# Sliding-window attention and a squared-ReLU MLP on one core: 64-column TensorE tiles, finer first units, token-by-token Q/K loads, V copies inside their partitions

## The chip, the cores and the metric

The kernel runs on one NeuronCore of a Trainium2 chip. The metric is device time in microseconds, the median of several executions. A profile is one more execution, recorded instruction by instruction. The engines are PE (TensorE, matmul; PEld is its weight load), DVE (VectorE), ACT (ScalarE), POOL (GpSimd, here mostly the issuer of casting loads from DRAM) and SP (SyncE, here the issuer of stores and of copies within SBUF).

## The reference

```python
def _attn_ref(q, k, v):            # 8 batches, 8 heads, 576 tokens, 64 wide, float32
    scores = scale * np.matmul(q, k.transpose(0, 1, 3, 2))      # scale = 1/8
    mask = np.abs(pos[:, None] - pos[None, :]) <= 32
    scores = np.where(mask, scores, -1000000000.0)
    ... softmax over the last axis ...
    return np.matmul(attn, v)
def _moe_ref(x, w_in, w_out):      # x 4608 x 512, w_in 512 x 2048, w_out 2048 x 512
    r = np.maximum(x @ w_in, 0.0)
    return (r * r) @ w_out
def reference(...):
    x = attn_out.transpose(0, 2, 1, 3).reshape(B * S, H * D)
    return _moe_ref(x=x, ...)
```

## The kernel before, in words

**Units.** Attention runs in 72 steps, n = 9b + c: batch b, 64 queries from token 64c, all eight heads, against the 128 keys that surround them. The MLP, called MoE in the code, runs in nine tiles T of 512 tokens, so one tile needs the output of eight steps.

**A step.** `scores` makes four matmuls of 128 keys by 128 (two heads of 64 queries each; QZ holds each head's queries in one half of the partitions and zeros in the other half, so that one matmul serves two heads). ACT takes exp of the 128x512 result (L484), DVE multiplies by a band mask into PT (L491). `av` makes eight matmuls (L506, L507): PT has 64 zero columns between its two heads, and each matmul takes 128 columns of it, one head and zeros, and adds to the same output AVP; V has a column of ones, so the sum of weights comes out beside the product. DVE takes the reciprocal (L522) and scales (L524). `xturn` transposes the result for the MoE: on PE and ACT for n below NPE = 28 (L542, L546), by a transposing DMA from SP afterwards.

**V.** Odd steps read V from VD as it was loaded (keys from token 32 on, 128 per slot). Even steps need keys that start 64 further, so `copy_v` copies VD to VX with the two halves of the partitions exchanged, by DMAs that SP issues (L401 to L411).

**Q and K.** For batches 0 and 1, `fine_load` brings 192 tokens at a time with four tokens of one head side by side in a partition (packets of 512 bytes), and `fine_turn` transposes them with 16 small PE transposes (L344) and four strided copies on ACT or DVE (L360, L363). Their scratch lies in buffers that are used for other things later. For batches 2 to 7, `load_qk` loads, `turn` transposes 32x32 blocks on DVE (L434), and `spread` moves the blocks to KT and QZ by SP DMAs.

**MoE.** `mm1` makes one 128-row block d of the hidden layer for 512 tokens (four matmuls of 128x512, L584), then relu on ACT and the square on DVE. Tiles 0 and 1 use `mm1_small` instead: four blocks for 128 tokens, 16 matmuls of 128x128 (L561). `mm2` makes a quarter of the sum for 128 output tokens (four matmuls of 128x512, L602); four of these make an output tile, in two alternating PSUM buffers, copied out by ACT (L611) and stored by SP.

**Order.** No order is written out. `Prog.rec` records every operation with a planned duration and a key; `Prog.schedule` is a list scheduler that gives each engine the ready operation of the lowest key. Attention steps have key n - LEAD and the MoE 8T + d/2, so LEAD is how many steps the attention runs ahead. Where the plan leaves PE idle in the first 36 us, `schedule` puts matmuls on zeros (L277) that keep its clock up. DMAs of POOL are in the order of keys in `build`. Each engine then runs its list in order and waits on semaphores.

Of the kernel before, what the change touches and what calls it, by code (L numbers as in the profile page):

```python
# [20 lines left out]
LEAD = 12  # L21
WARM = 36000
NPE = 28
NSMALL = 2
TOFF, TST, TREL = 6, 0.9, 9
NQ = 48
PC = 4 * NQ


class Op:  # L30
    __slots__ = ("eng", "fn", "deps", "order", "inc", "val", "sem", "dma", "dur", "key", "i",
                 "succ", "left", "ready", "start", "end", "lat", "move", "gate", "pos")


class Prog:
# [13 lines left out]
    def rec(self, eng, fn, reads=(), writes=(), dma=None, dur=100, key=0.0, move=0, old=(), gate=None, pos=None):  # L49
        op = Op()  # L50
        op.eng, op.fn, op.dma, op.dur, op.key, op.move = eng, fn, dma, dur, key, move
        op.gate, op.pos = gate, pos
# [23 lines left out]
    def schedule(self):  # L76
# [19 lines left out]
        out, held, reached = [], [], -100  # L96
# [42 lines left out]
        while True:  # L139
# [22 lines left out]
            op.start = t  # L162
            free[e] = t + op.dur
# [12 lines left out]
        at = free["PE"] = 1500  # L176
        for op in sorted((o for o in out if o.eng == "PE"), key=lambda o: o.start):
            gap = min(op.start, WARM, self.idle_end.start) - at
            one = 430 if at < 5000 else 230
            for k in range(int((gap - 60) // one)):  # L180
                w = Op()
                w.eng, w.fn, w.dma, w.deps, w.i = "PE", self.idle, None, {self.idle_on}, op.i
                w.inc, w.val, w.sem, w.start, w.end, w.dur, w.key = False, None, None, at + one * k, 0, one, -99
                out.append(w)
            at = max(at, op.start + op.dur)
# [43 lines left out]
class Gen:  # L229
# [5 lines left out]
    def alloc(self):  # L235
# [8 lines left out]
        self.RAW = {t: [sb(f"{t}raw{i}", [128, 9, 4, 64], BF16) for i in range(2)] for t in "qk"}  # L244
# [5 lines left out]
        self.MASK = [sb(f"mask{i}", [128, 64], BF16) for i in range(3)]  # L250
        self.ID = sb("ident", [128, 128], BF16)
        self.E = [sb(f"e{i}", [128, 512], BF16) for i in range(2)]
        self.PT = [sb(f"pt{i}", [128, 4 * 192], BF16) for i in range(2)]
        self.RS = [sb(f"rs{i}", [128, 4], F32) for i in range(2)]
        self.XR = [sb(f"xr{i}", [128, 256], BF16) for i in range(4)]
        self.XT = sb("xt", [128, NSTEP, 4, 64], BF16)
# [11 lines left out]
    def sel(self, t, name, pat, base, cm, key):  # L268
        self.p.rec("POOL", lambda e: e.affine_select(out=t[:], in_=t[:], pattern=pat, compare_op=ALU.is_ge,
                                                     fill=0.0, base=base, channel_multiplier=cm),  # L270
                   reads=[name], writes=[name], key=key, dur=270)

    def setup_idle(self):

        self.ms("DVE", ["zz"], self.ZZ[:], 0.0, -1000, 200)
        self.p.idle_on = self.p.ops[-1]
        self.p.idle = lambda e: e.matmul(self.OUTP[1][:], self.ZZ[:, 0:128], self.ZZ[:], start=True, stop=True)  # L277

    def setup_id(self, key):
        self.ms("DVE", ["id"], self.ID[:], 1.0, key)  # L280
        self.sel(self.ID, "id", [[-1, 128]], 0, 1, key)
        self.sel(self.ID, "id", [[1, 128]], 0, -1, key)

    def setup_mask(self, i, key):
        m = self.MASK[i]
        self.ms("DVE", [("mask", i)], m[:], 1.0, key)
        self.sel(m, ("mask", i), [[-1, 64]], 0, 1, key)
        self.sel(m, ("mask", i), [[1, 64]], 64, -1, key)
        if i == 1:
            self.sel(m, ("mask", 1), [[0, 64]], -32, 1, key)  # L290
        if i == 2:
            self.sel(m, ("mask", 2), [[0, 64]], 95, -1, key)

    def setup_rest(self, i, key):

        for s, r in ((0, 0), (4, 64)):
            t = [("vx", i, s)]
            self.ms("DVE", t, self.VX[i][r:r + 64, s, :, 0:64], 0.0, key, 280)
            self.ms("DVE", t, self.VX[i][r:r + 64, s, :, 64:VS], 1.0, key, 80)
        self.ms("DVE", [("vx", i, 0)], self.VX[i][64:128, 0, :, 64:VS], 1.0, key, 80)  # L300
# [4 lines left out]
    def setup_ptz(self, i, key):  # L305
        for j in range(4):
            self.ms("DVE", [("ptz", i)], self.PT[i][:, 192 * j + 64:192 * j + 128], 0.0, key, 70)

    def setup_qz(self, i, key, rows, old=()):

        for r, n, hm in rows:
            self.ms("DVE", [("qz0", i, r)], self.QZ[i][r:r + n, :, 1 - hm, :], 0.0, key, 1100, old)


    def fine_raw(self, b, t, x):

        if b == 0:
            if t == "q" or x == 0:
                return self.GT[1], 8192, 2048 * (x if t == "q" else 3)
            return self.RAW["q" if x == 1 else "k"][0], 2304, 0  # L320
        if x == 0:
            return self.RAW[t][1], 2304, 0
        return self.XT, 4 * NTOK, 256 * 40 + 2048 * (2 * (x - 1) + (t == "k"))

    def fine_load(self, b, t, x, key):
        h, row, base = self.fine_raw(b, t, x)
        src = (self.q if t == "q" else self.k)[b]
        s = src[:, PC * x:PC * x + PC, :].rearrange("h (p t) d -> p h (t d)", t=4)
        d = bass.AP(h, base, [[row, NQ], [256, 8], [1, 256]])
        self.p.rec("POOL", lambda e: e.dma_start(d, s), writes=[("fraw", b, t, x)], dma=(f"f{b}{t}{x}", 0), key=key,  # L330
                   dur=640, move=(24, 48))

    def fine_turn(self, b, t, x, key):

        h, row, base = self.fine_raw(b, t, x)
        tag, ps = ("sc", t == "q"), self.SC[t == "q"][:].bitcast(BF16)

        def f(e):
            for hm in range(2):
                for j in range(4):  # L340
                    for uu in range(2):
                        at = base + 256 * (4 * (j // 2) + 2 * hm + j % 2) + 128 * uu
                        to = NQ * (8 * hm + 2 * j + uu)
                        mm = e.transpose(ps[:, to:to + NQ], bass.AP(h, at, [[row, NQ], [1, 128]]), self.ID[0:NQ, 0:NQ])  # L344
            return mm

        self.p.rec("PE", f, reads=[("fraw", b, t, x), "id"], writes=[tag], key=key, dur=16 * 50)
        for hm in range(2):
            for par in range(2):
                src = ps[64 * par:64 * par + 64, 8 * NQ * hm:8 * NQ * hm + 8 * NQ].rearrange(  # L350
                    "p (j u q) -> p j q u", j=4, u=2)
                if t == "q":
                    dst = bass.AP(self.QZ[b], 64 * hm * 8 * S_ + hm * S_ + PC * x + par,
                                  [[8 * S_, 64], [2 * S_, 4], [4, NQ], [2, 2]])
                else:
                    dst = bass.AP(self.KT[b], 64 * hm * 4 * KW + 32 + PC * x + par,
                                  [[4 * KW, 64], [KW, 4], [4, NQ], [2, 2]])
                w = (t + "f", b, x, hm)
                if t == "q" or (b and x):
                    self.p.rec("ACT", lambda e, d=dst, c=src: e.activation(d, c, ACTF.Copy),  # L360
                               reads=[tag] + ([w] if par else []), writes=[w], key=key, dur=590)
                else:
                    self.p.rec("DVE", lambda e, d=dst, c=src: e.tensor_copy(d, c),  # L363
                               reads=[tag] + ([w] if par else []), writes=[w], key=key, dur=590)


    def load_qk(self, b, t, key):
        src = (self.q if t == "q" else self.k)[b]
        raw = self.RAW[t][b % 2]
        old = [("fraw", 0, "k", 1 if t == "q" else 2)] if b == 2 else []  # L370
        old += [("fraw", 1, t, 0)] if b == 3 else []
        for g in range(4):
            s = src[2 * g:2 * g + 2, :, :].rearrange("h s d -> (h s) d").rearrange(
                "(m r j) d -> r m j d", r=32, j=4)
            self.p.rec("POOL", lambda e, g=g, s=s: e.dma_start(raw[32 * g:32 * g + 32], s),
                       writes=[("raw", t, b % 2, g)], old=old, dma=(f"{t}{b % 2}", b), key=key, dur=610, move=(18, 48))
# [8 lines left out]
    def load_ve(self, b, key, hi):  # L385
        i = b % 2
        v = self.v
        if hi:
            self.p.rec("POOL", lambda e: e.dma_start(
                self.VX[i][64:96, 4, :, 0:64], v[b, :, 544:576, :].rearrange("h p d -> p h d")),  # L390
                writes=[("vx", i, 4)], dma=(f"ve{i}", b), key=key, dur=650, move=(16, 14))
        elif b < 2:
            self.p.rec("POOL", lambda e: e.dma_start(
                self.VX[i][32:128, 0, :, 0:64], v[b, :, 0:96, :].rearrange("h p d -> p h d")),
                writes=[("vx", i, 0)], dma=(f"ve{i}a", b), key=key, dur=800, move=(48, 14))
        else:
            self.p.rec("POOL", lambda e: e.dma_start(
                self.VX[i][32:64, 0, :, 0:64], v[b, :, 0:32, :].rearrange("h p d -> p h d")),
                writes=[("vx", i, 0)], dma=(f"ve{i}", b), key=key, dur=650, move=(16, 14))

    def copy_v(self, b, key, s0, s1):  # L401

        i = b % 2
        rd = [("vd", i, s) for s in range(s0, s1)] + [("vdone", i)]
        n = s1 - s0
        self.p.rec("SP", lambda e: e.dma_start(self.VX[i][0:64, s0 + 1:s1 + 1, :, :], self.VD[i][64:128, s0:s1, :, :]),
                   reads=rd, writes=[("vxl", i, s + 1) for s in range(s0, s1)], dma=(f"vx{i}{s0}{s1}", b), key=key,
# [339 lines left out]
```

## Time and profile before

| | us |
|---|---|
| median of 3 runs | 333.72 (333.63 to 334.93) |
| span of the profiled execution | 329.7 |
| PE, DVE, ACT, POOL busy | 312.8, 201.8, 172.8, 82.5 |
| mean granted TensorE clock | 0.995 |
| from HBM / to HBM | 36.96 MB / 9.44 MB |

The profiled execution's span runs from the first to the last instruction; the median of the timed runs is 4.0 us longer than it (333.72 - 329.7), which is taken as what lies around the span. A matmul's recorded duration contains its pipeline: a 128x512 matmul is recorded with 379 ns although the next one starts 216 ns later, so work on PE is counted below by the distance from start to start. PE is also recorded as busy while it runs the matmuls on zeros.

### The profile page before, as it was taken

Reading aid. Unit: us, or ns where it says so; the run is one execution under the profiler, and the core shown is the slowest. Engines: PE = TensorE matmul, PEld = TensorE weight load, DVE = VectorE, ACT = ScalarE, POOL = GpSimd, SP = SyncE. Lnnn points to the kernel's source line nnn. Section 1 sums busy time; section 2 is a strip of 40 time slices with the busy share of each in tenths; the row PEclk is TensorE's granted clock in tenths of the full one; section 3 lists DMA queues with packets and bytes.
Section 4 is the critical chain, followed back from the end, with each engine's and each line's share of the span. In section 5 each row is a group of like instructions: output and inputs, shape, how many; then the busy total and the mean of one; then the engine's idle time right before and its main releaser. Section 6 shows DMA issues by size and latency. Waiting matters only on the chain.

```text
span 329.7 us, 6908 instructions
## 1 busy us (share of the span) xinstructions
PE 312.8 (95%) x2707; PEld 176.9 (54%) x2707; DVE 201.8 (61%) x461; ACT 172.8 (52%) x313; POOL 82.5 (25%) x130
## 2 busy tenths in 40 slices
PE   7699897999799999989899999999999999999996
PEld 3356496786685555445455555555555554444442
DVE  7546564989689788779777767777544442222200
ACT  2366279965574764555264555554455554434411
POOL 8999253125053242405321110000000000000000
PEclk9989999999999999999999999999999999999999
DMA  8999999999999999799999668333311111100012
GB/s 92 173 202 203 193 150 184 182 237 199 213 184 164 210 144 126 94 224 172 173 196 150 125 123 148 89 85 84 86 49 48 51 55 55 43 32 34 32 72 88
DMA packets 89376, 42.53 MB, mean 129 GB/s; under 512 B 54528, under 2 KB 83840, under 8 KB 89344
## 3 DMA queue, kind: packets, MB, share of 16 engines
q0 software_dynamic: 62272, 18.49, 61.1%
q1 hardware_dynamic: 27072, 23.60, 28.2%
q8 instruction: 21, 0.34, 0.5%
q14 instruction: 11, 0.09, 0.1%
HBM read 36.96 MB, written 9.44 MB: 141 GB/s over the span
## 4 chain that ended last, share of the span: by engine, by line
PE 81%; DMA 7%; DVE 6%; ACT 2%; issue 1%; POOL 1%; SPq 1%; ACTq 0%
PE outp L602 34%; PE ht L584 28%; PE ht L561 7%; PE sc L479 5%; DMA qz<-qst 4%; DMA qraw<-in_k_dram 2%; PE avp L507 2%; PE avp L506 2%; DVE qz L266 2%; PE outp L277 1%; DMA xt<-xr 1%; PE sc L344 1%; PE trp L542 1%; DVE qst L434 1%; SPq L454 1%
## 5 line engine op out<-in xcount | busy, mean ns | idle before, releaser
L602 PE MATMUL outp<-w,gt 128*128 128x512 bf16 x576 | 143.1, 379 | 0.9 <-DVE gt L570 0.9
L584 PE MATMUL ht<-xt,w 128*128 128x512 bf16 x448 | 113.5, 379 | 0.9 <-DMA xt<-xr 0.9
L590 ACT ACTIVATE rt<-ht 128x512 bf16<-128x512 f32 x112 | 66.9, 597 | 80.9 <-PE ht L584 77.7
L602 PEld LDWEIGHTS outp<-w,gt 128*128 128x128 bf16 x576 | 53.7, 98 | 59.1 <-DVE gt L570 1.5
L592 DVE TENSOR_TENSOR gt<-rt 128x512 bf16<-128x512 bf16 x112 | 46.3, 420 | 50.0 <-ACT rt L590 49.4
L584 PEld LDWEIGHTS ht<-xt,w 128*128 128x128 bf16 x448 | 40.7, 98 | 40.1 <-DMA xt<-xr 1.4
L484 ACT ACTIVATE e<-sc 128x512 bf16<-128x512 f32 x72 | 41.6, 596 | 18.5 <-PE sc L479 12.4
L381 POOL DMA_DIRECT2D vd<-in_v_dram x32 | 28.8, 911 | 84.0 <-PE avp L507 63.3
L491 DVE TENSOR_TENSOR pt<-e,mask 128x512 bf16<-128x512 bf16 x72 | 29.9, 416 | 16.5 <-ACT e L484 15.9
L434 DVE STREAM_TRANSPOSE kst<-kraw 128x640 bf16<-128x640 bf16 (+1 forms) x24 | 35.0, 1457 | 0.6 <-DMA kt<-kst 0.6
L434 DVE STREAM_TRANSPOSE qst<-qraw 128x640 bf16<-128x640 bf16 (+1 forms) x24 | 35.1, 1462 | 0.0
L611 ACT ACTIVATE oe<-outp 128x512 f32<-128x512 f32 x36 | 21.6, 600 | 24.8 <-PE outp L602 24.8
L561 PE MATMUL ht<-xt,w 128*128 128x128 bf16 x512 | 32.8, 219 | 1.3 <-issue 0.7
L524 DVE TENSOR_TENSOR xr<-avp,rs 128x256 bf16<-128x256 f32 x72 | 30.2, 420 | 1.9 <-DVE rs L522 0.2
L522 DVE RECIPROCAL rs<-avp 128x4 f32<-128x4 f32 x72 | 13.2, 184 | 29.5 <-PE avp L507 28.8
L561 PEld LDWEIGHTS ht<-xt,w 128*128 128x128 bf16 x512 | 29.3, 98 | 3.4 <-ACT rt L567 1.2
L479 PE MATMUL sc<-qz,kt 128*128 128x128 bf16 x288 | 25.9, 219 | 4.9 <-DMA qz<-qst 3.4
L479 PEld LDWEIGHTS sc<-qz,kt 128*128 128x128 bf16 x288 | 19.8, 98 | 15.9 <-DMA qz<-qst 4.4
L567 ACT ACTIVATE rt<-ht 128x512 bf16<-128x512 f32 x32 | 19.0, 600 | 7.3 <-PE ht L561 6.3
L277 PE MATMUL outp<-zz 128*128 128x512 bf16 x59 | 18.0, 437 | 1.3 <-DVE zz L266 1.3
L360 ACT ACTIVATE qz<-sc 64x384 bf16<-64x384 bf16 x24 | 14.3, 596 | 9.3 <-PE sc L344 8.8
L506 PE MATMUL avp<-vx,pt 128*128 128x65 bf16 x160 | 15.1, 192 | 2.6 <-DMA vx<-in_v_dram 2.6
(51 smaller groups left out, 220.6 us busy)
## 6 DMA issues: line engine op xcount, KB each, us to landing
out_dram<-oe SPq DMA_DIRECT2D x36, 256.0 KB, 2.3
vd<-in_v_dram POOLq DMA_DIRECT2D x32, 128.0 KB, 8.2
qraw<-in_q_dram POOLq DMA_DIRECT2D x24, 144.0 KB, 7.4
kraw<-in_k_dram POOLq DMA_DIRECT2D x24, 144.0 KB, 8.3
qz<-qst SPq DMA_DIRECT2D x48, 72.0 KB, 3.5
kt<-kst SPq DMA_DIRECT2D x24, 144.0 KB, 4.6
vx<-vd SPq DMA_DIRECT2D x12, 264.0 KB, 4.9
w<-in_moe_w_in_dram POOLq DMA_DIRECT2D x4, 512.0 KB, 11.1
```

The costliest lines, as they stand in the source:

```text
L381: self.p.rec("POOL", lambda e, s=s: e.dma_start(self.VD[i][:, s, :, 0:64], v[b, :, 32 + 128 * s:160 + 128 * s, :].rearrange("h p d -> p h ...
L434: self.p.rec("DVE", lambda e: e.transpose(dst, src), reads=[("raw", t, i, g) for g in range(4)], writes=[("st", t, dh, m0)], key=key, dur= ...
L479: mm = e.matmul(sc[:, 128 * j:128 * j + 128], self.KT[i][:, j, 64 * c:64 * c + 128], self.QZ[i][:, j, :, 64 * c:64 * c + 64], start=True, ...
L484: self.p.rec("ACT", lambda e: e.activation(self.E[n % 2][:], sc[:], ACTF.Exp, scale=0.125), reads=[("sc", n % 2)], writes=[("e", n % 2)], ...
L491: self.p.rec("DVE", lambda e: e.tensor_tensor(pt, ee, mb, ALU.mult), reads=[("e", n % 2), ("mask", mi)], writes=[("pt", n % 2)], key=key, ...
L506: e.matmul(o, pt[:, 192 * j:192 * j + 128], vt[:, ha, 0:VE], start=True, stop=False)
L524: self.p.rec("DVE", lambda e: e.tensor_tensor(bass.AP(xr, 0, [[256, 128], [64, 4], [1, 64]]), bass.AP(self.AVP, 0, [[512, 128], [VE, 4], [ ...
L561: mm = e.matmul(ht[:, 128 * (d % 4):128 * (d % 4) + 128], self.W1[:, ft, 128 * d:128 * d + 128], self.XT[:, t0 // 64:t0 // 64 + 2, ft, :], ...
L584: mm = e.matmul(ht[:], self.W1[:, ft, 128 * d:128 * d + 128], self.XT[:, 8 * T:8 * T + 8, ft, :], start=(ft == 0), stop=(ft == 3))
L590: self.p.rec("ACT", lambda e: e.activation(rt[:], ht[:], ACTF.Relu), reads=[("ht", k % 2)], writes=[("rt", k % 4)], key=key, dur=560)
L592: self.p.rec("DVE", lambda e: e.tensor_tensor(gt[:, d, :], rt[:], rt[:], ALU.mult), reads=[("rt", k % 4)], writes=[("gt", T % 2, d, u) for ...
L602: mm = e.matmul(op[:], gt[:, d, 128 * u:128 * u + 128], self.W2[:, d, :], start=(d == 0), stop=(d == 15))
```

## The change

It changes six things together.

1. **Two 64-column tiles.** Nearly every matmul becomes two of 64 output partitions each, one for partitions 0 to 63 of PSUM and one for 64 to 127 (`matmul` with mode "col", and `scores`, `av`, `xturn`). In `scores` each half takes its own 64 keys, and for even c the halves are exchanged. In `av` one head goes to each half, so PT has no zeros between heads and each matmul has 64 columns instead of 128. Full-width matmuls remain in `fine_turn` and in seven units of tile 0. The scheduler adds SWITCH = 95 to its plan where two neighbours on PE have different modes.
2. **MoE units.** Tile 0 is made of seven units of 128 tokens and nine of 256 tokens in the order UNITS, tile 1 of 256-token units, the others of 512 as before.
3. **Q and K of batches 0 and 1** are loaded token by token (128 tokens on 128 partitions, all heads, packets of 128 bytes) and turned with four transposes of 128x128; K is copied once by DVE, Q twice by ACT with a factor of 1 or 0 for each half of the partitions (HALF), which also writes the zeros. They have buffers of their own (FR).
4. **V for even steps.** Because the halves of keys are exchanged, VX keeps V in the partitions where VD has it; `copy_v` is two DVE copies instead of two DMAs.
5. **Masks and identity** are made by one iota on POOL and compares, multiplies and copies on DVE, instead of eight selects on POOL.
6. **Order.** The first 40 loads follow the list FIRST. LEAD is 26, NPE 24; XT is a ring of 32 steps; `load_qk` takes 18 tokens of a head in a row per partition, `turn` works on nine blocks at a time, and other keys have other constants.

```diff
-LEAD = 12
+LEAD = 26
-NPE = 28
-NSMALL = 2
+NPE = 24
+RX = 32
+SWITCH = 95
+UNITS = (
+    (0, 128, 8), (128, 128, 0), (128, 128, 8), (0, 128, 0), (0, 128, 4), (128, 128, 4), (0, 128, 12),
+    (256, 256, 8), (128, 128, 12), (256, 256, 0), (256, 256, 12), (256, 256, 2), (256, 256, 4),
+    (256, 256, 10), (256, 256, 14), (256, 256, 6),
+)
+FIRST = (
+    ("q", 0, 0), ("a", 0, 1), ("e", 0, True), ("v", 0, 3), ("k", 0, 0), ("v", 0, 0), ("e", 0, False),
...
+    ("b", 0, 2), ("b", 0, 3),
+)
+PIECES = ((0, 128), (128, 128), (256, 128), (384, 128), (512, 64))
+def matmul(e, mode, out, w, x, start, stop):
+    if mode == "full":
+        return e.matmul(out, w, x, start=start, stop=stop)
+    for r in (0, 64):
+        mm = e.matmul(out[r:r + 64], w[:, r:r + 64], x, start=start, stop=stop)
+    return mm
...
+            if e == "PE" and op.mode != tiling:
+                op.dur += SWITCH
...
     def fine_load(self, b, t, x, key):
+        t0, n = PIECES[x]
+        s = (self.q if t == "q" else self.k)[b][:, t0:t0 + n, :].rearrange("h p d -> p h d")
+        d = self.FR[t][b][0:n, x, :, :]
...
     def fine_turn(self, b, t, x, key):
-                        mm = e.transpose(ps[:, to:to + NQ], bass.AP(h, at, [[row, NQ], [1, 128]]), self.ID[0:NQ, 0:NQ])
+            for j in range(4):
+                src = bass.AP(self.FR[t][b], 512 * x + 128 * j, [[2560, n], [1, 128]])
+                mm = e.transpose(ps[:, n * j:n * j + n], src, self.ID[0:n, 0:n])
+        if t == "k":
+            self.p.rec("DVE", lambda e: e.tensor_copy(dst, src), ...)
+            return
+        for hm in range(2):
+            self.p.rec("ACT", lambda e, d=dst, hm=hm: e.activation(d, src, ACTF.Copy, scale=self.HALF[:, hm:hm + 1]), ...)
...
     def copy_v(self, b, key, s0, s1):
-        self.p.rec("SP", lambda e: e.dma_start(self.VX[i][0:64, s0 + 1:s1 + 1, :, :], self.VD[i][64:128, s0:s1, :, :]),
+        for r in (0, 64):
+            self.p.rec("DVE", lambda e, r=r: e.tensor_copy(self.VX[i][r:r + 64, s0 + r // 64:s1 + r // 64, :, :],
+                                                           self.VD[i][r:r + 64, s0:s1, :, :]), ...)
...
     def scores(self, n):
-                mm = e.matmul(sc[:, 128 * j:128 * j + 128], self.KT[i][:, j, 64 * c:64 * c + 128],
-                              self.QZ[i][:, j, :, 64 * c:64 * c + 64], start=True, stop=True)
+                for u in range(2):
+                    at = 64 * c + 64 * (u if c % 2 else 1 - u)
+                    mm = e.matmul(sc[64 * u:64 * u + 64, 128 * j:128 * j + 128], self.KT[i][:, j, at:at + 64],
+                                  self.QZ[i][:, j, :, 64 * c:64 * c + 64], start=True, stop=True)
...
     def av(self, n):
-                e.matmul(o, pt[:, 192 * j:192 * j + 128], vt[:, ha, 0:VE], start=True, stop=False)
-                mm = e.matmul(o, pt[:, 192 * j + 64:192 * j + 192], vt[:, ha + 2, 0:VE], start=False, stop=True)
+                for u in range(2):
+                    h = 4 * (j // 2) + j % 2 + 2 * u
+                    mm = e.matmul(self.AVP[64 * u:64 * u + 64, VE * j:VE * j + VE], pt[:, 64 * h:64 * h + 64],
+                                  vt[:, h, 0:VE], start=True, stop=True)
...
+    def mm1(self, T, t0, n, d0, key, mode="col"):
+        nd, s0 = 512 // n, 8 * T + t0 // 64
+            for d in range(nd):
+                for ft in range(4):
+                    mm = matmul(e, mode, ht[:, n * d:n * d + n], self.W1[:, ft, 128 * (d0 + d):128 * (d0 + d) + 128],
+                                self.XT[:, x0:x0 + n // 64, ft, :], ft == 0, ft == 3)
...
     def mm2(self, T, u, seg, key):
+                mm = matmul(e, "col", op[:], gt[:, d, 128 * u:128 * u + 128], self.W2[:, d, :], d == 0, d == 15)
...
+    def tile(self, T):
+        if T == 0:
+            for t0, n, d0 in UNITS:
+                self.mm1(0, t0, n, d0, KM + 0.01 * self.k1, "full" if n == 128 else "col")
+            return
```

More of the change, by code (lines that the diff above doesn't have):

```diff
@@ L175, in schedule @@
         assert len(out) == len(ops)
-        at = free["PE"] = 1500
+        at, last = 1500, "full"
         for op in sorted((o for o in out if o.eng == "PE"), key=lambda o: o.start):
@@ L294, in setup_rest @@
-    def setup_rest(self, i, key):
[L296 to L300, printed above, removed]
+        self.p.idle = {m: lambda e, m=m: matmul(e, m, self.OUTP[1][:], self.ZZ[:, 0:128], self.ZZ[:], True, True)
+                       for m in ("full", "col")}
@@ new lines, in setup_ramp @@
+    def setup_ramp(self, key):
+        p = self.p
+        p.rec("POOL", lambda e: e.iota(self.RAMP[:], [[-1, 128]], base=0, channel_multiplier=1,
+                                       allow_small_or_imprecise_dtypes=True), writes=["ramp"], key=key, dur=270)
+        p.rec("DVE", lambda e: e.tensor_scalar(self.ID[:], self.RAMP[:], 0.0, None, ALU.is_equal),
+              reads=["ramp"], writes=["id"], key=key, dur=160)
+        for hm in range(2):
+            for r in range(4):
+                self.ms("DVE", ["half"], self.HALF[32 * r:32 * r + 32, hm:hm + 1], float(r // 2 == hm), key, 70)
@@ L303, in setup_rest @@
         self.ms("DVE", [("ktpad", i, 1)], self.KT[i][:, :, 32 + S_:KW], 0.0, key)
[L305 to L323, printed above, removed]
@@ L333, in fine_turn @@
     def fine_turn(self, b, t, x, key):
-        h, row, base = self.fine_raw(b, t, x)
+        t0, n = PIECES[x]
         tag, ps = ("sc", t == "q"), self.SC[t == "q"][:].bitcast(BF16)
         def f(e):
[L339 to L344, printed above, removed]
-            return mm
@@ new lines, in f @@
+            return mm
+        self.p.rec("PE", f, reads=[("fraw", b, t, x), "id"], writes=[tag], key=key, dur=4 * 58 if n == 128 else 4 * 30,
+                   mode="full" if n == 128 else "row")
+        src = ps[:, 0:4 * n].rearrange("p (j c) -> p j c", j=4)
+        if t == "k":
+            dst = self.KT[b][:, :, 32 + t0:32 + t0 + n]
+            self.p.rec("DVE", lambda e: e.tensor_copy(dst, src), reads=[tag], writes=[("kf", b, x, 0)], key=key,
+                       dur=690 if n == 128 else 420)
+            return
@@ L594, in mm1 @@
+        us = range(t0 // 128, (t0 + n) // 128)
+        self.p.rec("DVE", lambda e: e.tensor_tensor(gt[:, d0:d0 + nd, t0:t0 + n], rr, rr, ALU.mult),
+                   reads=[("rt", k % 4)], writes=[("gt", T % 2, d0 + d, u) for d in range(nd) for u in us], key=key,
                    dur=430)
@@ L660, in build @@
-        self.fine_load(1, "q", 2, K + 34)
-        self.load_v(1, K + 35, 2)
-        self.load_v(1, K + 36, 3)
-        self.load_ve(1, K + 36, True)
+        self.setup_rest(1, -6)
+        load = {"k": lambda b, x, k: self.fine_load(b, "k", x, k), "q": lambda b, x, k: self.fine_load(b, "q", x, k),
+                "v": self.load_v_at, "e": lambda b, x, k: self.load_ve(b, k, x),
+                "a": lambda b, x, k: self.load_w1(x, k), "b": lambda b, x, k: self.load_w2(x, k)}
+        for i, (what, b, x) in enumerate(FIRST):
+            load[what](b, x, K + i)
@@ L695, in build @@
                 self.xturn(n)
[L697 to L708 removed]
+                if n % 8 == 7 and n > 15:
+                    self.tile(n // 8 - 2)
+        for T in range(NT - 2, NT + 1):
+            self.tile(T)
         p.schedule()
```

362 lines of the change are left out of this document (131 added, 231 removed), and 4 rows, old and new, of the table FIRST.

## The prediction

> **What bounds the kernel now.** I read the page's costliest groups first, then PE's groups in the first 40 us, then the chain of waits between 40 and 50 us for the distance from start to start. The page's groups (name, operation, count, then busy us and mean ns) give PE's whole work:
>
> ```profile
> span 329.7 us, 6908 instructions
> ...
> L602 PE MATMUL outp<-w,gt 128*128 128x512 bf16 x576 | 143.1, 379 | 0.9 <-DVE gt L570 0.9
> L584 PE MATMUL ht<-xt,w 128*128 128x512 bf16 x448 | 113.5, 379 | 0.9 <-DMA xt<-xr 0.9
> ...
> L561 PE MATMUL ht<-xt,w 128*128 128x128 bf16 x512 | 32.8, 219 | 1.3 <-issue 0.7
> ...
> L479 PE MATMUL sc<-qz,kt 128*128 128x128 bf16 x288 | 25.9, 219 | 4.9 <-DMA qz<-qst 3.4
> ...
> L506 PE MATMUL avp<-vx,pt 128*128 128x65 bf16 x160 | 15.1, 192 | 2.6 <-DMA vx<-in_v_dram 2.6
> ```
>
> The chain of waits, in order of time (start, us, what), gives what one costs when PE is fed:
>
> ```profile
> 41.13 0.11 PE trp L542 x2
> ...
> 43.39 0.03 PE avp L506
> ...
> 43.63 1.79 PE ht L561 x32
> 45.42 0.90 PE sc L344 x32
> 46.32 0.28 PE trp L542 x2
> 46.59 1.79 PE ht L561 x32
> 48.38 0.86 PE outp L602 x4
> 49.24 0.45 PE sc L479 x8
> ...
> 311.94 14.69 PE outp L602 x68
> ```
>
> So a 128x512 matmul costs 216 ns (14.69/68), a 128x128 one 56 (1.79/32; scores 0.45/8), a transpose of L344 28 (0.90/32), one of L542 55, and one of av 30.5 (eight between 43.39 and 43.63). A step has eight of av, so 576 (the row of 160 is one of four), 56 of L542 (28 steps by two) and 192 of L344 (two batches, three pieces, Q and K, 16 each). Work: 1024 x 0.216 = 221.2; 512 x 0.056 = 28.7; 288 x 0.056 = 16.1; 576 x 0.0305 = 17.6; 56 x 0.055 = 3.1; 192 x 0.028 = 5.4; together 292.1 us. The span has 329.7, so 37.6 us are lost: PE is the bound, and any gain is either work removed or one of these 37.6. Where are they? PE's groups of the first 40 us:
>
> ```profile
> L277 PE MATMUL outp<-zz 128*128 128x512 bf16 x59 | 18.0, 437 | 1.3 <-DVE zz L266 1.3
> L561 PE MATMUL ht<-xt,w 128*128 128x128 bf16 x64 | 4.3, 219 | 0.2
> L602 PE MATMUL outp<-w,gt 128*128 128x512 bf16 x16 | 3.9, 379 | 0.3 <-DVE gt L570 0.3
> L479 PE MATMUL sc<-qz,kt 128*128 128x128 bf16 x36 | 3.0, 219 | 0.2 <-ACT qz L360 0.2
> L542 PE MATMUL trp<-ident,xr 128*128 128x128 bf16 x12 | 1.8, 233 | 1.2 <-DVE xr L524 1.1
> ```
>
> With 56 of av and 96 of L344 that is 3.6 + 3.5 + 2.0 + 0.7 + 1.7 + 2.7 = 14.2 us of work in 40: 25.8 lost, most of it under 59 matmuls on zeros. The windows view (busy us of each engine, clock, DMA share, GB/s) shows the rest:
>
> ```profile
> 0.00:40.00 40.00, 33.24 (x339) 18.57 (x339) 23.92 (x73) 17.72 (x32) 33.66 (x58) 0.96 1.32 174
> 40.00:100.00 60.00, 55.25 (x844) 44.69 (x845) 45.77 (x94) 43.94 (x86) 20.45 (x31) 1.00 1.74 193
> 100.00:165.00 65.00, 62.69 (x499) 33.51 (x498) 53.40 (x114) 34.75 (x66) 22.26 (x33) 1.00 1.18 162
> 165.00:270.00 105.00, 105.00 (x769) 54.70 (x766) 67.76 (x158) 54.93 (x95) 6.14 (x8) 1.00 0.52 100
> 270.00:326.60 56.60, 56.60 (x263) 25.45 (x261) 10.96 (x26) 20.89 (x35) 0.00 (x0) 1.00 0.13 48
> ```
>
> PE idles 4.75 us between 40 and 100 and 2.3 between 100 and 165, never from 165 to 326.6; behind that stand 3.1 us for the last copy and store. 25.8 + 4.75 + 2.3 + 3.1 = 36, the 37.6 within rounding; the missing 1.6 go to the stage 40 to 100 (6 there). Three of those later waits, from PE's timeline:
>
> ```profile
> 87.56 0.62 PE L479 MATMUL sc<-qz,kt 128*128 128x128 bf16 x8 [2.00 <-DMA qz<-qst]
> 143.72 0.62 PE L479 MATMUL sc<-qz,kt 128*128 128x128 bf16 x8 [1.42 <-DMA qz<-qst]
> 163.79 1.02 PE L584 MATMUL ht<-xt,w 128*128 128x512 bf16 x4 [0.90 <-DMA xt<-xr]
> ```
>
> **The change part by part.** The trace has no matmul on half of the columns. Everything hangs on what a pair of them costs: at best one full matmul (the halves run beside each other), at worst two.
>
> *MoE and scores, in pairs.* Twice the instructions, the same columns. I take a pair as one matmul of the same length, 216 and 56 ns: cost 0. The other end is two in a row: +221 us for the 512-column ones, +21.6 for the 25 of 256, +16 for scores.
>
> *av.* Before, eight matmuls with half of their columns zeros; now four pairs of 65 columns. As pairs: 4 x 30.5 = 122 ns a step instead of 244, times 72: -8.8 us. Other end: each half has an interval of its own, by the nearest small matmul L344's 28 ns: 8 x 28 = 224, -1.4 us. I take -8.8, as for the other pairs.
>
> *Transposes and first tiles.* `fine_turn` goes from 192 x 0.028 = 5.4 to 72 x 0.056 + 8 x 0.028 = 4.3; `xturn` on PE from 28 steps to 24, -0.4. Tiles 0 and 1 go from 28.7 to seven units of 16 x 0.056 and 25 of 4 x 0.216, 27.9. Together -2.3.
>
> *Changes of layout.* In the built order PE changes between full and half tiles 41 times, 23 of them before the first `mm2`, where it waits anyway. A change can cost from 0 to the tail of a matmul that is then no longer covered, 219 - 56 = 163 ns by the scores' row: 0 to 2.9 us for the other 18; I take half, +1.5. [...]
>
> *The first 60 us.* Loads of batches 0 and 1 and both weights are, as stored in bf16, 2.36 (Q, K) + 1.18 (V) + 4.19 = 7.7 MB. The last two quarters of W2 are now the last of the forty in FIRST, so everything must land before tile 0's sums can end. Rates:
>
> ```profile
> 20.00:30.00 10.00, 9.52 (x119) 5.77 (x117) 5.56 (x13) 5.88 (x12) 10.00 (x15) 1.00 1.52 197
> 40.00:50.00 10.00, 9.93 (x181) 9.02 (x182) 6.38 (x17) 7.09 (x15) 5.12 (x9) 1.00 2.68 150
> ...
> vd<-in_v_dram POOLq DMA_DIRECT2D x32, 128.0 KB, 8.2
> vx<-vd SPq DMA_DIRECT2D x10, 66.0 KB, 5.8
> ...
> L381 POOL DMA_DIRECT2D vd<-in_v_dram x32 | 28.8, 911 | 84.0 <-PE avp L507 63.3
> ```
>
> 197 GB/s where weights and 512-byte packets dominate, 150 where V's 128-byte packets do. Q and K now come in such packets too, four times as many; in return the V copies (some 0.9 MB here) leave the DMA. 7.7 MB take 39 to 51 us; from about 3 us on and with some 2 to land, the last weight is there at 44 to 56: no earlier than before. POOL issues the 40 loads at up to 0.9 us each (L381), 36 us, in front of that. So the fill isn't shorter; what differs is what PE finds meanwhile. In the built order, ahead of the run of eight `mm2` groups that wants all of W2, stand batch 0's and most of batch 1's attention, tile 0 and seven units of tile 1: 39.6 us of work by the prices above. ACT's work up to there goes by these rows and its share by the windows:
>
> ```profile
> L484 ACT ACTIVATE e<-sc 128x512 bf16<-128x512 f32 x72 | 41.6, 596 | 18.5 <-PE sc L479 12.4
> L360 ACT ACTIVATE qz<-sc 64x384 bf16<-64x384 bf16 x24 | 14.3, 596 | 9.3 <-PE sc L344 8.8
> L546 ACT ACTIVATE xt<-trp 128x256 bf16<-128x256 bf16 x28 | 10.7, 383 | 12.7 <-PE trp L542 12.4
> ...
> 50.00:60.00 10.00, 7.90 (x140) 6.57 (x139) 4.82 (x12) 9.50 (x20) 2.58 (x4) 1.00 1.76 191
> ```
>
> 23 relus and 18 exps of 128x512 at 0.6, 16 xt copies at 0.38, 20 Q copies at 0.6 (as L360, whose 384 columns lie between their 512 and 256), two output copies at 0.6: 44 us, from the first Q at about 6 us on. ACT ran at 44% in the first 40 us, at 73% from 40 to 100, at 95% in its fullest 10 us. At 100% the run of eight starts at 50, at 73% at 66; I take 83%, 59 us, since attention 26 instead of 12 steps ahead leaves ACT more that is ready. Lost until then: 59 - 39.6 = 19.4. Before, the same work was done with 25.8 + 6 x (39.6 - 14.2)/54 = 28.6 lost, at 68 us. Gain 9, from 2 (66 us) to 18 (50 us).
>
> *Later.* The waits for qz and xt sum to 4.3 in the three rows; with 14 more steps of lead I take away half of what is lost between there and 165 (4.5): -2.3; bounds 0 and -4.3. The tail's 3.1 stays.
>
> *What I cost at nothing.* V copies on DVE, by the square's row:
>
> ```profile
> L592 DVE TENSOR_TENSOR gt<-rt 128x512 bf16<-128x512 bf16 x112 | 46.3, 420 | 50.0 <-ACT rt L590 49.4
> ```
>
> 2112 columns at 512 in 0.42 us are at most 1.7 us each, 3.4 a batch, two batches between 100 and 165, where DVE has 11.6 us free; without that room up to 6.9 us would reach PE. Masks on DVE fall before the first K. `turn` makes 96 pieces of 9 blocks out of 48 of 16 or 20: the same blocks. `spread` issues 16 DMAs a batch where 12 and two V copies were; what is queued behind them on SP, the transposing DMAs for xt, has 14 more steps of time; if that isn't enough, a wait like the 0.90 us for xt above comes back, six batches of it 5.4 us.
>
> Sum: -8.8 - 2.3 + 1.5 - 9 - 2.3 = -20.9. Span 329.7 - 20.9 = 308.8; with 4.0 around it, 312.8, so **313 us**.
>
> **The rivals.**
>
> *A. The fill gains nothing.* Loads of 128-byte packets are slow (150 GB/s, 51 us), ACT no fuller than 73%, and the new order's gain is eaten by its waits. -8.8 - 2.3 + 1.5 - 0 = -9.6: 324. For it: the same bytes and no earlier last weight; against it: 59 matmuls on zeros show how much work of batch 1 could be drawn forward.
>
> *B. Halves of av don't overlap.* -1.4 in place of -8.8: 320. For it: at 28 to 30 ns a small matmul may be bound by its issue; against it: nothing in the trace.
>
> *C. Slower: narrow weight loads.* Each half loads 64 columns of weights, and the two loads of a pair can't hide behind a short matmul.
>
> ```profile
> L479 PEld LDWEIGHTS sc<-qz,kt 128*128 128x128 bf16 x288 | 19.8, 98 | 15.9 <-DMA qz<-qst 4.4
> ```
>
> A load is recorded with 98 ns, hidden now behind 30.5 ns matmuls because several are under way. If a pair must spend 98 ns: scores 288 x 42 = 12.1, av 288 x (98 - 30.5) = 19.4, xturn 48 x 42 = 2.0, on the forecast: +33.5, **346 us**. 512- and 256-column pairs (216, 108 ns) still cover it. It decides once a short pair costs 33 ns more than forecast (20.9/624 pairs): 64 for av, 89 for scores. Against it: today's loads are pipelined threefold. [...]
>
> *D. The halves run one after the other:* +221, +21.6 and +16, and av back to 244 ns, +8.8: 313 + 267 = 580. Then "two tiles" would not do what it says.
>
> **How the numbers follow.** Forecast 0.58, its own range 304 to 319 (fill gain 2 to 18, with half of the ends of layout and later). A 0.17, B 0.13, C 0.10, D 0.02. The range 303 to 328 takes in A and B with A's DVE and layout ends, and leaves out C, D and a little below: 0.2. Half a percent, 1.7 us, is what a measurement of this kernel tells from no change. Faster by more: the forecast, A and B less 0.03 for A's upper end, 0.85; within: 0.03; slower: C, D, 0.12.
>
> **What would show it.** Right: pairs of 512 columns 216 ns apart, av's eight in about 0.12 us, scores' in 0.22; the run of eight `mm2` groups starting near 60 us; no PE idle to speak of after 100. B shows as eight of av in 0.22; C as 98 or more between pairs of scores; A as that run starting past 66. It fails altogether if a 512-column pair takes more than 236 ns: 20 ns on 1024 pairs are the whole gain.

## The result and the profile after

The changed kernel takes 343.5 us (median of 4 runs) against 333.7 before: 1.027 times as long (95% interval 1.021 to 1.033). Forecast were 313 us and "faster". The span is 341.5 us.

The page of the kernel after (shares of the chain of waits that ended last, then the costliest groups):

```profile
DVE 44%; PE 41%; DMA 5%; issue 5%; POOL 2%; ACT 2%; SPq 1%; DVEq 0%; ACTq 0%
...
L52 PE MATMUL outp<-w,gt 128*64 128x512 bf16 x1152 | 140.2, 381 | 0.4 <-DVE gt L560 0.4
...
L430 DVE STREAM_TRANSPOSE kst<-kraw 128x288 bf16<-128x288 bf16 x48 | 65.5, 1469 | 0.1
L430 DVE STREAM_TRANSPOSE qst<-qraw 128x288 bf16<-128x288 bf16 x48 | 64.6, 1501 | 0.0
...
L470 PE MATMUL sc<-qz,kt 128*64 128x128 bf16 x576 | 25.7, 222 | 7.6 <-DMA qz<-qst 6.7
...
L410 DVE COPY vx<-vd 64x528 bf16<-64x528 bf16 (+1 forms) x28 | 16.7, 597 | 4.1 <-DMA vd<-in_v_dram 3.5
```

The chain now runs through DVE as much as through PE, and two rows say why. `turn` at L430 transposes 96 pieces of 288 columns, which take 1.47 and 1.50 us each, 130 us together. Before, 48 turns of 640 and 512 columns took 70 us, although they turned just as many columns (by form, kernel before):

```profile
L434 DVE STREAM_TRANSPOSE qst<-qraw 128x640 bf16<-128x640 bf16 x12 | 19.3, 1607 | 0.0
L434 DVE STREAM_TRANSPOSE kst<-kraw 128x640 bf16<-128x640 bf16 x12 | 19.2, 1598 | 0.6 <-DMA kt<-kst 0.6
L434 DVE STREAM_TRANSPOSE kst<-kraw 128x512 bf16<-128x512 bf16 x12 | 15.8, 1316 | 0.0
L434 DVE STREAM_TRANSPOSE qst<-qraw 128x512 bf16<-128x512 bf16 x12 | 15.8, 1316 | 0.0
```

A block below means 32 columns on all 128 partitions (four squares of 32x32 beside each other), as in the prediction. A block costs 1607/20 = 80 ns there and 1485/9 = 165 ns after (1485 is the mean of the two rows), each with its share of what a turn has recorded beside its blocks (148 ns by the line through the two sizes before, 1316 - 16 x 73). The windows of the kernel after, by the prediction's stages (busy us of PE, PEld, DVE, ACT, POOL, clock, DMA share, GB/s), show where that bites:

```profile
40.00:100.00 60.00, 53.15 (x880) 39.41 (x877) 53.67 (x100) 32.60 (x65) 18.29 (x28) 0.94 1.10 158
100.00:165.00 65.00, 56.43 (x692) 30.53 (x692) 62.53 (x114) 31.48 (x56) 16.16 (x26) 0.97 0.80 128
165.00:270.00 105.00, 96.73 (x1279) 56.92 (x1274) 96.63 (x195) 54.67 (x96) 13.01 (x19) 1.00 0.58 102
```

DVE is nearly full from 100 to 165 us (62.5 of 65), and PE idles 8.6 us there and 8.3 in the next stage, where it idled 2.3 and 0 before. The longest wait, in DVE's and PE's timeline:

```profile
57.69 10.09 DVE L430 STREAM_TRANSPOSE kst<-kraw 128x288 bf16<-128x288 bf16 x8
67.44 10.20 DVE L430 STREAM_TRANSPOSE qst<-qraw 128x288 bf16<-128x288 bf16 x8
...
60.57 1.03 PE L52 MATMUL outp<-w,gt 128*64 128x512 bf16 x8
...
78.28 0.42 PE L529 MATMUL trp<-ident,xr 128*64 128x128 bf16 x4 [6.29 <-DVE xr L511]
...
78.73 1.90 PE L52 MATMUL outp<-w,gt 128*64 128x512 bf16 x8
```

Sixteen turns in a row hold DVE for 20 us. The squares and the scaling for PE queue behind them, and PE stands still for 6.3 us. The wait has a second price. The next eight matmuls of 512 columns are recorded with 1.90 us, where eight of them took 1.03 at 60.57, and the granted clock (the 0.50 below) is one half there and once more later:

```profile
75.30:82.10 6.80, 3.82 (x36) 2.56 (x38) 5.32 (x13) 1.85 (x4) 3.03 (x5) 0.50 0.69 140
123.00:126.40 3.40, 3.40 (x38) 2.00 (x36) 2.42 (x7) 2.18 (x5) 0.06 (x1) 0.51 0.27 65
```

The second stretch comes 1.2 us after a wait of 2.00 us for Q's copies. PE is busy for 7.2 of these 10.2 us, so by estimate they cost half of that, 3.6 us, beside the waits themselves.

The pairs, on which the prediction put its doubts, do what was hoped. The chain of waits of the kernel after, near 50 us:

```profile
47.70 0.33 PE sc L359 x4
48.03 0.99 PE ht L52 x16
...
50.45 0.13 PE avp L497 x8
50.58 0.23 PE sc L470 x8
50.80 0.86 PE outp L52 x8
```

Eight half matmuls of 512 columns take 0.86 us, as four full ones did; eight of av 0.13 instead of 0.24; eight of scores 0.23. The four full transposes between half matmuls take 0.33 us instead of 0.22, and the 16 half matmuls behind them 0.99 instead of 0.86: a change of layout costs about 0.1 us each way.

### The profile page after: what moved, and what is told of

The parts are those of the page before. It is cut to its first block, busy times and chain, and to the rows that moved or that the text cites. A ratio compares the mean times of both kernels' runs of the same rounds, so it can differ in the third digit from the quotient of the medians.

```text
span 341.5 us, 9457 instructions
## 1 busy us (share of the span) xinstructions
PE 309.3 (91%) x3952; PEld 184.5 (54%) x3952; DVE 252.5 (74%) x529; ACT 164.5 (48%) x297; POOL 86.3 (25%) x129
## 4 chain that ended last, share of the span: by engine, by line
DVE 44%; PE 41%; DMA 5%; issue 5%; POOL 2%; ACT 2%; SPq 1%; DVEq 0%; ACTq 0%
PE outp L52 16%; PE ht L52 16%; DVE qst L430 15%; DVE kst L430 13%; DVE gt L560 5%; DVE xr L511 4%; DMA qz<-qst 3%; DVE pt L482 3%; PE sc L470 2%; PE ht L50 2%; DMA vd<-in_v_dram 2%; DVE rs L509 2%; PE avp L497 1%; PE sc L359 1%; DVE vx L410 1%
## 5 line engine op out<-in xcount | busy, mean ns | idle before, releaser
L52 PE MATMUL outp<-w,gt 128*64 128x512 bf16 x1152 | 140.2, 381 | 0.4 <-DVE gt L560 0.4
L52 PE MATMUL ht<-xt,w 128*64 128x512 bf16 (+1 forms) x1280 | 135.7, 351 | 0.2 <-issue 0.2
L560 DVE TENSOR_TENSOR gt<-rt 128x512 bf16<-128x512 bf16 x144 | 61.5, 445 | 42.1 <-ACT rt L556 34.5
L52 PEld LDWEIGHTS ht<-xt,w 128*64 128x64 bf16 x1280 | 70.5, 111 | 40.4 <-ACT rt L556 2.2
L52 PEld LDWEIGHTS outp<-w,gt 128*64 128x64 bf16 x1152 | 64.1, 110 | 50.0 <-DVE gt L560 0.8
L430 DVE STREAM_TRANSPOSE kst<-kraw 128x288 bf16<-128x288 bf16 x48 | 65.5, 1469 | 0.1
L430 DVE STREAM_TRANSPOSE qst<-qraw 128x288 bf16<-128x288 bf16 x48 | 64.6, 1501 | 0.0
L470 PE MATMUL sc<-qz,kt 128*64 128x128 bf16 x576 | 25.7, 222 | 7.6 <-DMA qz<-qst 6.7
L509 DVE RECIPROCAL rs<-avp 128x4 f32<-128x4 f32 x72 | 18.5, 256 | 12.7 <-PE avp L497 12.6
L470 PEld LDWEIGHTS sc<-qz,kt 128*64 128x64 bf16 x576 | 19.7, 111 | 12.8 <-DMA qz<-qst 5.1
L410 DVE COPY vx<-vd 64x528 bf16<-64x528 bf16 (+1 forms) x28 | 16.7, 597 | 4.1 <-DMA vd<-in_v_dram 3.5
```

The source lines that it names most:

```text
L52: mm = e.matmul(out[r:r + 64], w[:, r:r + 64], x, start=start, stop=stop)
L430: self.p.rec("DVE", lambda e: e.transpose(dst, src), reads=[("raw", t, i, g) for g in range(4)], writes=[("st", t, dh, h2, x)], key=key, d ...
L470: mm = e.matmul(sc[64 * u:64 * u + 64, 128 * j:128 * j + 128], self.KT[i][:, j, at:at + 64], self.QZ[i][:, j, :, 64 * c:64 * c + 64], star ...
L509: self.p.rec("DVE", lambda e: e.reciprocal(rs[:], bass.AP(self.AVP, 64, [[512, 128], [VE, 4]])), reads=["avp"], writes=[("rs", n % 2)], ke ...
L560: self.p.rec("DVE", lambda e: e.tensor_tensor(gt[:, d0:d0 + nd, t0:t0 + n], rr, rr, ALU.mult), reads=[("rt", k % 4)], writes=[("gt", T % 2 ...
```

## The experiments

Theory 1: the turn costs by the stride of its output (18 elements now, 4 before), DVE has too much to do, and that is the whole loss. Rivals: the new order and the V copies on DVE (theory 2), or the scheduler's wrong duration for the turn (theory 3).

### The stride alone

The control loads each head by itself, so that a partition can hold J consecutive tokens of a head, J = 18, 6, 2 or 1; the turn's output then has stride J. The order of work is one and the same for all four on every engine. What changes beside the stride is the order of the blocks, how many of them a turn has, and the packets of the loads, which only get smaller with J.

```diff
-            d = raw[32 * g:32 * g + 32].rearrange("p h i d -> p h (i d)")
+            for x in range(2):
+                s = src[h + 2 * x].rearrange("(m r j) d -> r m (j d)", r=32, j=J)
+                d = raw[32 * g:32 * g + 32, x].rearrange("p (m j) d -> p m (j d)", j=J)
...
-        src = bass.AP(raw, 1152 * h2 + 576 * x + 32 * dh, [[2304, 128], [64, 9], [1, 32]])
-        dst = bass.AP(st, 1152 * dh + 576 * h2 + 9 * x, [[2304, 128], [1, 9], [18, 32]])
+        src = bass.AP(raw, 1152 * h2 + 64 * J * m0 + 32 * dh, [[2304, 128], [64 * J, n], [64, J], [1, 32]])
+        dst = bass.AP(st, 1152 * dh + 576 * h2 + 32 * J * m0, [[2304, 128], [32 * J, n], [1, J], [J, 32]])
```

J = 18, the control:

> The changed kernel with one load per head (eight of 32 partitions instead of four of two heads) for Q and K of batches 2 to 7; same addresses in SBUF, same turn with output stride 18. Control for the next two. Both theories: like the changed kernel, 338 to 347 us, a turn of 9 blocks about 1.45 us.

Measured: 339.6 us, 1.020 times before (1.011 to 1.030). Against the changed kernel this is 3.9 us less by the medians; loading by head also makes the scheduler plan another order, and the two aren't told apart. So the runs below are compared with the control.

J = 6:

> As the control, but a partition holds 6 tokens of a head side by side instead of 18, so turn writes with stride 6 elements (12 bytes) instead of 18 (36 bytes). Theory 1 (turn costs by the stride of its output, and DVE so bound sets the time): a block between the 81 ns of stride 4 (8 bytes, before) and the 163 ns of stride 18, time between the control and the next one. Theory 2 (the stride does not matter for the time; the new order and the DVE copies of V do): within 1% of the control.

Measured: 321.0 us in one run. By form:

```profile
L432 DVE STREAM_TRANSPOSE qst<-qraw 128x384 bf16<-128x384 bf16 x24 | 36.0, 1501 | 0.0
...
L432 DVE STREAM_TRANSPOSE qst<-qraw 128x192 bf16<-128x192 bf16 x24 | 20.6, 856 | 0.0
```

Six blocks more cost 645 ns: 108 a block, and by the line through these two sizes some 210 more are recorded for a turn. Against the control, 18.6 us are gone, most of the way to the next one; theory 2 said 1%.

J = 2:

> As the control, with 2 tokens side by side: turn writes with stride 2 elements (4 bytes). Engines' order of work is that of the control. Theory 1: a block at or below 81 ns, so 96 turns cost at most 70 us instead of 130, DVE busy at most 195 us instead of 252, no PE waits to speak of from 100 us on, 308 to 318 us. Theory 2: turn may be faster, but the time stays above 335 us.

Measured: **316.5 us, 0.951 times before** (0.943 to 0.959). Turns by form, then the windows and DVE's timeline:

```profile
L432 DVE STREAM_TRANSPOSE kst<-kraw 128x320 bf16<-128x320 bf16 x24 | 12.6, 525 | 0.0
...
L432 DVE STREAM_TRANSPOSE kst<-kraw 128x256 bf16<-128x256 bf16 x24 | 10.8, 450 | 0.0
```

```profile
40.00:100.00 60.00, 59.63 (x998) 50.17 (x994) 40.69 (x121) 36.95 (x75) 41.49 (x65) 1.00 1.63 194
100.00:165.00 65.00, 62.02 (x800) 37.26 (x798) 45.11 (x130) 34.69 (x61) 32.62 (x52) 1.00 1.20 139
165.00:270.00 105.00, 104.21 (x1310) 70.18 (x1307) 62.48 (x178) 58.17 (x101) 5.76 (x8) 1.00 0.45 87
```

```profile
57.17 3.01 DVE L432 STREAM_TRANSPOSE kst<-kraw 128x320 bf16<-128x320 bf16 x8
60.08 2.98 DVE L432 STREAM_TRANSPOSE qst<-qraw 128x320 bf16<-128x320 bf16 x8
```

Two blocks more cost 75 ns, 38 a block. The sixteen turns that held DVE for 20 us are over in 6; the 96 together take 43.7 us (both sizes in one row each):

```profile
L432 DVE STREAM_TRANSPOSE kst<-kraw 128x320 bf16<-128x320 bf16 (+1 forms) x48 | 22.4, 488 | 0.0
...
L432 DVE STREAM_TRANSPOSE qst<-qraw 128x320 bf16<-128x320 bf16 (+1 forms) x48 | 21.3, 478 | 0.0
```

PE idles 0.4, 3.0 and 0.8 us in the three stages. The stride is worth 23 us against the control, where nothing else of the order differs, and with the loads by head 27 against the changed kernel. The rest of the change is a gain.

J = 1:

> As e3_s2 with one token per place, so turn writes with stride 1 element (2 bytes) and the loads have packets of 128 bytes. [...]

Measured: 319.1 us in one run.

```profile
L432 DVE STREAM_TRANSPOSE kst<-kraw 128x288 bf16<-128x288 bf16 x48 | 21.5, 463 | 0.0
```

Nine blocks in 463 ns lie on the line of J = 2 (450 for eight, 525 for ten: 488 for nine), a little below. So 2 bytes gain nothing over 4.

### The same on the kernel before

```diff
-                "(m r j) d -> r m j d", r=32, j=4)
+            s = src[2 * g:2 * g + 2, :, :].rearrange("h s d -> (h s) d").rearrange("(r i) d -> r (i d)", r=32)
...
-        dst = bass.AP(st, dh * 1152 + 128 * m0, [[2304, 128], [128, n], [1, 4], [4, 32]])
+        dst = bass.AP(st, dh * 1152 + 4 * m0, [[2304, 128], [1, 4 * n], [36, 32]])
```

> The kernel before, with load_qk taking 36 tokens in a row per partition and turn writing with stride 36 elements (72 bytes) instead of 4; nothing else. Theory 1: a block 163 ns or more instead of 81, the 48 turns 140 us instead of 70, DVE busy near 270 us, and the kernel 10 to 25 us slower, 343 to 358. Theory 2: at most 340.

Measured: 359.3 us, 1.079 times before (1.070 to 1.088).

```profile
L433 DVE STREAM_TRANSPOSE qst<-qraw 128x640 bf16<-128x640 bf16 x12 | 35.7, 2975 | 0.0
...
L433 DVE STREAM_TRANSPOSE qst<-qraw 128x512 bf16<-128x512 bf16 x12 | 28.9, 2409 | 0.0
```

142 ns a block, less than the 163 expected, and still 26 us, 1 us above the expected range: the wide stride alone makes the kernel before slower by more than the whole change does. The other way round, two tokens in place of four:

> The kernel before with two tokens side by side instead of four, so that turn writes with stride 2 elements instead of 4; its order of work is unchanged. Theory: turns fall from 70 to about 45 us, but DVE does not bound the kernel before, so only its waits for qz (4.3 us in its trace) can shrink: 329 to 334 us, and the rest of the gain of e3_s2 is the other parts of the change. Rival: short turns alone are most of e3_s2's gain; then below 326.

Measured: 333.2 us against 333.4, ratio 1.000 (0.996 to 1.004).

```profile
L435 DVE STREAM_TRANSPOSE qst<-qraw 128x640 bf16<-128x640 bf16 x12 | 10.7, 890 | 0.0
```

The 640-column turns fall from 1607 to 890 ns, and nothing comes of it: DVE was not the bound. So shorter turns alone are worth nothing, and the other parts make the gain of the stride-2 kernel over the one before. Of its 17 us, 12.7 are there at J = 6 already (333.7 - 321.0), with 108 ns a block where the kernel before pays 73. How the changed kernel would do with just the stride of before was not run.

### The planned duration

The scheduler of the changed kernel reckons with 740 for a turn that takes 1480.

```diff
-                   dur=740, gate=gate)
+                   dur=1480, gate=gate)
```

> The changed kernel itself (stride 18, four loads) with turn's planned duration 1480 instead of 740, as it takes. Theory 1 (DVE has too much to do between 60 and 250 us): the planner spreads the turns better, but DVE stays near 250 us busy: 325 to 340. Theory 3 (the loss is the planner's error, since it puts twice the turns that fit ahead of urgent work): 320 or less.

Measured: 370.1 us, 1.110 times before (1.100 to 1.121): worse than not knowing by 27 us, outside both. DVE is 260 us busy, and the last scores start at 304.8 us instead of 265.9. Theory 3 falls. The profiled span is 24.0 us longer than that of the changed kernel. PE is idle for 46.9 us of it instead of 32.2 (span less PE's busy time), and the granted clock is one half for 34.1 us, the longest stretch being this:

```profile
144.20:157.90 13.70, 4.75 (x42) 2.66 (x44) 8.18 (x18) 1.19 (x2) 3.92 (x6) 0.50 1.21 137
```

PE is busy for 22.6 of the 34.1 us, which by the same estimate costs 11.3 us instead of 3.6. Together that is 14.7 + 7.7 of the 24.0 us. Why this plan makes PE wait more is not settled; the other keys and gates were set with 740.

On the stride-2 kernel, 500 and 1000:

> The stride-2 kernel (e3_s2) with turn's planned duration 500 instead of 740, near what it takes there (444 to 521 ns). If the plan's wrong duration still costs something, 1 to 4 us faster than e3_s2; if the planner's slack makes no difference, within 1 us of it (315 to 318).

> The stride-2 kernel with turn's planned duration 1000 instead of 740. Theory (a planned duration above the true one is slack for the copies that spread starts, which land later than planned; at the true 500 PE waited 11.9 us for qz): 314 to 318 us. Rival (any re-planning shuffles the order for worse): 320 or more.

Measured: 322.5 us (0.969, 0.960 to 0.977) and 322.6 us (0.971, 0.965 to 0.977), both 6 us behind 740. At 500 both expectations missed; at 1000 the rival came, that a re-plan makes it worse. At 500 PE waits for Q's copies, six times, 11.9 us in all, against 2.6 in the stride-2 kernel (PE's waits: total, times, longest):

```profile
PE sc L472 <- DMA qz<-qst: 11.9, 6, 4.8
```

At 1000 this is 1.3 us, and the loss lies elsewhere, between 80 and 140 us, where PE idles 6.6 us instead of 1.1. A re-plan moves the time by 6 us, which is the size of what the smaller parts of the change are worth; this stays open.

### The pairs and the changes of layout

```diff
-                mm = matmul(e, mode, ht[:, n * d:n * d + n], ...
+                mm = matmul(e, "full", ht[:, n * d:n * d + n], ...
-                mm = matmul(e, "col", op[:], gt[:, d, 128 * u:128 * u + 128], ...
+                mm = matmul(e, "full", op[:], gt[:, d, 128 * u:128 * u + 128], ...
```

> The stride-2 kernel with every matmul of the MoE on all 128 columns again, attention in halves, the same order. The layout changes 198 times on PE instead of 41. Theory: a pair costs what a full matmul does and a change costs 96 ns, as e3_s2's trace shows where a full and a half matmul meet (150 ns from start to start instead of 56); 157 more changes on an engine that is the bound: 15 us slower, 329 to 333. [...]

Measured: 329.5 us, 0.987 times before (0.979 to 0.996), 13.0 us behind the stride-2 kernel by the medians and 12.0 by the two ratios to the kernel before: 76 to 83 ns for each of 157 changes. That fits the 0.1 us read from the chain, and leaves no price for the pairs; so halves in the MoE gain nothing by themselves but save the changes of layout.

### The fill

```diff
-    ("q", 0, 0), ("a", 0, 1), ("e", 0, True), ("v", 0, 3), ("k", 0, 0), ("v", 0, 0), ("e", 0, False),
-    ("k", 0, 1), ("q", 0, 1), ("v", 0, 2), ("k", 0, 2), ...
+    ("q", 0, 0), ("k", 0, 0), ("v", 0, 0), ("e", 0, False),
+    ("k", 0, 1), ("q", 0, 1), ("a", 0, 1), ("e", 0, True), ("v", 0, 3), ("v", 0, 2), ("k", 0, 2), ...
```

> The stride-2 kernel with the first K, V and V edge ahead of the first quarter of W1 in FIRST (q, k, v, edge, k, q, then W1). Theory (the fill starts late because the first K lands only 8.0 us after its issue, behind 1 MB of W1): scores begin near 8 us instead of 14.3, 2 to 5 us faster than e3_s2: 311.5 to 314.5. Rival (the fill is set by all bytes and by ACT later on): within 1 us of e3_s2.

Measured: 318.4 us, 0.955 times before (0.945 to 0.965). The first scores start 5.6 us earlier (PE's timeline, this kernel):

```profile
8.66 0.41 PE L472 MATMUL sc<-qz,kt 128*64 128x128 bf16 x8 [0.91 <-ACT qz L372]
```

but by 60 us PE has done the same work as in the stride-2 kernel, 35 us of it counted at the prediction's prices, so the first K does not set the fill. Both expectations missed: the median is 1.9 us behind the stride-2 kernel, though the single runs of the two overlap (316.4 to 320.7 and 315.4 to 317.8).

```diff
-LEAD = 26
+LEAD = 12
```

> The stride-2 kernel with LEAD 12 instead of 26, re-planned. Theory (the 26 steps of lead are what fills PE early and covers later landings): 320 us or more, with more waits for xt or qz. Rival (the lead is worth nothing once DVE is free): 314 to 319.

Measured: 315.8 us, 0.951 times before (0.945 to 0.958): the rival. Twelve steps of lead do as well as 26, and the fill is the same too: 39.6 us of PE's work are done at 64.3 us here and at 65.0 with 26. This and the stride-2 kernel are the fastest found; they can't be told apart.

## Why the prediction was wrong, point by point

**The step that failed** stands under "What I cost at nothing": "`turn` makes 96 pieces of 9 blocks out of 48 of 16 or 20: the same blocks." The blocks are the same and their output isn't: stride 18 instead of 4. The term was 0 and measured 60 us of DVE (130 against 70). In time, the control gives back 18.6 us at J = 6 and 23 at J = 2 (339.6 against 321.0 and 316.5); the prediction's silent assumption, a stride of 4 as before, lies between the two and was not run. The prediction had DVE free for 11.6 us between 100 and 165 us and spent that on V copies; it quoted no row for the turn. The before row's 1607 ns for 640 columns are 2.5 ns a column, where the square's row, quoted there, pays 0.8 (420/512): a hint that the access pattern might set the price, and the diff changes just that pattern.

**Rival C named the right time for the wrong reason.** It said 346, but its mechanism, narrow weight loads, is refuted: PEld is recorded with 110 ns a load, and eight half matmuls of scores still take 0.23 us. The runs show no cost of the narrow loads down to 65 columns. B and D fall with the same rows: eight of av in 0.13 us, 512-column pairs at 216 ns.

**The other terms**, read from the stride-2 kernel, which has all of the change but the stride (and loads by head). First two miscounts that hardly change the sum. UNITS holds eight units of 128 tokens and eight of 256, not seven and nine, so with tile 1 there are 24 units of 256 tokens instead of 25, and 8 x 16 x 0.056 + 24 x 4 x 0.216 is 27.9 all the same. `fine_turn` makes 64 long and 16 short transposes, not 72 and 8, which is 0.2 us less. All matmuls of the trace at the prediction's prices are 280.7 us against 292.0 before, -11.3 where -8.8 and -2.3 were forecast: right.

A change of layout costs 0.08 (from the MoE on full tiles, 12.0 to 13.0 us for 157 changes) to 0.1 us (from the chain), inside the bounds of 0 and 0.163 and near the half that was taken.

The fill gained 3.6 us where 9 were forecast. The run of eight `mm2` groups, for which 59 us were forecast, starts at 65.0 (PE's timeline, stride-2 kernel):

```profile
64.95 7.15 PE L52 MATMUL outp<-w,gt 128*64 128x512 bf16 x64
```

At that point 39.6 us of work are done, so 25.4 are lost; the kernel before had that work done at 68.6, with 29.0 lost. The assumption that ACT would be 83% busy failed: from 6 to 65 us it is busy for 39.9 of 59 us, 68%. That is what rival A said of ACT, yet A's sum, no gain at all, is not what came. The reason given for the fuller ACT, the lead, is refuted by LEAD 12; what did bring the 3.6 us is not shown. "Later" gained 0.1 us where 2.3 were forecast (5.2 lost from there to 300 us, before 5.3). Lost in all: 33.8 us, the changes of layout among them, against 37.7 before.

**The sum.** -11.3 of work and -3.9 of loss give the span of 314.5, 5.7 us more than the 308.8 forecast. The stride-2 kernel's median is 2.0 us above its profiled span where 4.0 were put in, so 316.5 instead of the 318.5 that this sum would say. In every execution on record the time is 1.7 to 1.9 us above that same execution's span; the 4.0 compared the median before with the span of another, faster execution. So 313 comes within 3.5 us of the change without its largest error, in part by luck: the fill and "later" promised too much, and the 4.0 gave 2 us back.

V copies were bounded at 3.4 us of DVE a batch. In the changed kernel the 12 copies of 2112 columns took 0.73 us each, 1.5 a batch; the 16 shorter ones of batches 0 and 1 took 7.9, so 4 a batch. With the turns short, PE idles only 3.0 us between 100 and 165 us with these copies in place.

## What to carry to other kernels

When an operation keeps its size and only its access pattern changes, price it by the pattern: divide a row's time by its columns, and where that is far above what other rows of the engine pay, measure what the pattern costs before widening its stride. A list scheduler's durations are not neutral facts: the measured ones, put in afterwards, made two plans worse, and so did one that nobody had measured (1000). And a part of a large change is only judged when the others are held still: the other parts were worth 4 to 5% all along, behind a stride that cost 7%.

## What the runs showed of the hardware

A block of bf16 in the DVE transpose (32 columns on all partitions), by the stride of its output, from the difference between two sizes in the same run. At 36 bytes there is one size only, so the changed kernel's eight turns in a row serve: (10.09 - 1.47)/7 = 1.23 us from one to the next, 137 ns a block. The rest of a turn's recorded 1.47 us lies under the next turn.

| output stride, bytes | 4 | 8 | 12 | 36 | 72 |
|---|---|---|---|---|---|
| ns a block | 38 | 73 | 108 | 137 | 142 |

From 4 to 12 bytes the price goes up by 35 ns for every 4 bytes, about in proportion to the stride. It hardly grows from 36 to 72 bytes (137 and 142), and at 2 bytes it does not fall much further: nine blocks took 463 ns, where the line of 4 bytes has 488. Continued at 35 ns for 4 bytes, the first three prices reach 137 to 142 at 15.3 to 15.9 bytes; that is an estimate from these prices, for no stride between 12 and 36 bytes was run, and why the price stops growing is not shown. Among the kernels of one family (the one before and its variants, or the control and J = 6 and 2), only the output's stride, the order and number of the blocks and the packets of the loads differ.

Two half matmuls on the two column halves cost one full matmul, at 512, 128 and 65 columns alike (0.86 us for eight halves of 512, 0.23 of 128, 0.13 of 65), and a change between full and half layout about 0.1 us. Behind PE's waits of 6.3 and 2.0 us the changed kernel shows a granted clock of one half, for 6.8 and 3.4 us; the stride-2 kernel, without these waits, shows it only once, for 3.4 us from 13.8 us on, just behind a wait of 2.42 us for the first K, and the kernel before once, for 3.4 us from 15.6 us on, 1.6 us after a wait of 2.56 us for V.
